# A fused attention and two-MLP kernel on one core: loads of the opening reordered, the scheduler's constants set anew, first copies of the seven products on two engines

## The chip, the cores and the metric

The kernel runs on one core of one Trainium2 chip. The metric is device time of one execution in microseconds (us), as the median of several runs.

## What is computed

```python
a = softmax(phi, axis=2)                        # phi: 4 batches, 8 heads, 576 rows, 32 memory slots
k_m = einsum('bhsm,bhsd->bhmd', a, k)           # k, v, q: 4, 8, 576, 64
v_m = einsum('bhsm,bhsd->bhmd', a, v)
attn = softmax(q @ k_m.T / sqrt(64)) @ v_m
x = attn.transpose(0, 2, 1, 3).reshape(2304, 512)
h = x @ w_in                                    # 512 x 2048
y = maximum(0.01 * h, h) @ w_out                # 2048 x 512
out = ((y @ w_a) * (y @ w_b)) @ w_out2          # 512 x 1536 twice, 1536 x 512
```

All of it is in fp32; softmax subtracts the row's maximum and adds 1e-9 to the sum.

## The kernel before

Every large matrix product runs on TensorE (PE) as three passes over operands that are split into a high and a low part (`hi` and `lo`). A weight arrives as 64-bit words; `weight` (to L525) loads it (L475, queue SP), turns it to fp32 in five passes (L481 and L484 on ACT, L488, L492, L496 and L499 on VectorE, DVE), and splits it: the high part is a copy (L404 or L406), the low part a subtraction (L505 on DVE, L387 on GpSimd, POOL).

The attention comes first. The batch index is b = 0 to 3, a head group g = 0 or 1 holds four heads, x = 0 or 1 is a half of 288 of the 576 rows. `kv_part(b, g)` loads phi, k with v (two tiles `kv` and a rest `kvr`), takes the softmax of phi (L555, L556, L559 and L560), transposes it (`ta`, `tz`), makes k_m and v_m (`km`), scales them (`kvn`, L595), transposes them (`kvt`) and sets them out (`kbd`, `vm_hi`, `vm_lo`). `q_load` loads q. `sc_part(b, g, x)` makes the scores (`sc`, L674), and on DVE their softmax: L680 (transposition), L688, L689, L693 to L695, L698, L699 (transposition back), then the split into `ahi` and `alo` (L705). `vw` multiplies v_m with w_in, so that the first MLP's h is the attention weights times `vw`, split again into `vwh` and `vwl` (L745, L772). The first MLP is in four chunks c of 512 columns; in each, `h_unit` makes h of block n (block n is batch n // 2, half n % 2) and leaky values `g` (L783, L822), and `y_unit` adds the products with w_out. The second MLP is in twelve chunks of 128 columns and two halves s of the rows; `ab_unit` makes its two products by seven products of half matrices, `o_unit` multiplies by w_out2. In half s = 1 the first eight chunks take w_out2 by seven products as well: `w2_sums` loads a tile `wf` (L1163) and makes sums of its quarters (`w2s`, `w2`), `p_sums` those of the other side (`pf`, `pT`, `pb`), and `o_part` multiplies (`os`, L1248). The results of the first pair of chunks are copied to seven tiles `osum`, each with two halves x (L404 on ACT or L406 on DVE), later ones are added.

The order of all this isn't written out. Every operation is handed to a `Program` with its engine (or several to choose from), its cost in us, what it reads and writes, and the tiles it holds. `urgency` goes back from the planned times of the main products and gives each operation a latest start, less its `slack`; `order` then places the operations one by one, on each engine the most urgent of those that are ready, and among several engines the one that would end first; `run` makes six rounds of that and keeps the shortest plan. `ahead` says how long before its latest start an operation may run, `keep` how many free slots must be left by it. Slots of 4 KB are handed out in that plan as well, 24 of them called `slot` and 20 called `big`; a load that takes a slot waits until its last reader is done, and a store is such a reader. `SLACK` holds the slacks by kind, `START` is the time planned for the first main product, `BIAS` is added to the cost of a copy on DVE. What comes out is five fixed lists of instructions, four engines and one queue of transfers (SP).

```python
def copy_by(n, psum=False):
    return (dict if psum else Port)({"ACT": c_act(n), "DVE": (c_dve(n) if psum else c_dve2(n)) + BIAS})
```

Of the kernel before, what the change touches and what calls it, by code (L numbers as in the profile page):

```python
# [19 lines left out]
P = 128  # L20
# [60 lines left out]
def c_dma(nbytes):  # L81
    return max(0.6, nbytes / 355e3)
# [250 lines left out]
def tile_mem_attention__leaky_mlp__bilinear_mlp(  # L333
# [128 lines left out]
    def weight(kind, c, k, after=()):  # L462
# [61 lines left out]
        op(copy_by(512), 0, hi, r=[a], w=[("hi", key)], tiles=[cv, key], ahead=any_time)  # L524
        op(two(512), 0, lo, r=[a, ("hi", key)], w=[key], tiles=[cv, key], ahead=any_time, slack=SLACK[kind + "0" if first else kind])  # L525


    def kv_part(b, g):
# [119 lines left out]
    def q_load(b, g):  # L648
# [584 lines left out]
    def o_part(q, x, nth, pos):  # L1233
# [151 lines left out]
```

## Time and profile before

| what | before |
|---|---|
| median of 3 runs | 809.02 us (807.88 to 809.16) |
| the profiled execution, own time | 809.07 us |
| its span in the trace | 807.3 us |
| PE busy | 784.9 us, 97% |
| DVE busy | 667.7 us, 83% |
| ACT busy | 375.8 us, 47% |
| POOL busy | 215.2 us, 27% |

The span is the time from the first to the last instruction of the trace; the execution's own time is 1.8 us longer. Busy time counts work only: an engine that waits for a transfer, or for another engine, is idle. Since PE does the bulk of the work in a fixed amount, its idle time is where time can be won, and what ended each piece of idle time is the question to ask of every view.

### The profile page before, as it was taken

How to read it: one execution, taken by the hardware profiler on the slowest of the kernel's cores; microseconds unless marked ns; L12 is line 12 of the kernel's file. 1: busy time of each engine (PE TensorE's matmuls, PEld its weight loads, DVE VectorE, ACT ScalarE, POOL GpSimd, SP SyncE). 2: the span in 40 equal slices, each digit the busy share in tenths (PEclk: the TensorE clock that was granted, in tenths of full speed). 3: DMA queues.
4: the chain of work that ended last, by engine and by line, in shares of the span. 5: the costliest groups of instructions: out<-in, count | busy, mean ns of one | idle time of the engine just before them, and what ended most of it. 6: DMA issues, size and time to landing. Idle time of an engine off the chain costs nothing.

```text
span 807.3 us, 13391 instructions
## 1 busy us (share of the span) xinstructions
PE 784.9 (97%) x4898; PEld 700.0 (87%) x4898; DVE 667.7 (83%) x1273; ACT 375.8 (47%) x817; POOL 215.2 (27%) x328
## 2 busy tenths in 40 slices
PE   5889999999999999999999999999999989999998
PEld 4578889999999999999988888888888878878886
DVE  6898899889887988888768899889885676888975
ACT  5657776777565665654326534344321143222110
POOL 3462247215011411431100113056330000244300
PEclk9789999999999999999999999999999999999999
DMA  9885302064227133136887555646578778957302
GB/s 325 323 281 181 132 1 74 6 235 125 76 76 267 59 132 118 42 125 233 279 311 276 209 199 192 208 158 202 216 264 304 276 267 274 296 173 283 130 1 104
DMA packets 55218, 150.02 MB, mean 186 GB/s; under 512 B 6897, under 2 KB 20209, under 8 KB 55153
## 3 DMA queue, kind: packets, MB, share of 16 engines
q1 hardware_dynamic: 55152, 149.18, 53.4%
q8 instruction: 38, 0.62, 0.3%
q14 instruction: 28, 0.22, 0.1%
HBM read 103.55 MB, written 45.61 MB: 185 GB/s over the span
## 4 chain that ended last, share of the span: by engine, by line
PE 93%; DMA 3%; DVE 2%; issue 1%; ACT 0%; SPq 0%; DVEq 0%; ACTq 0%
PE y L836 26%; PE o L1132 13%; PE h L806 12%; PE aby L1049 12%; PE abz L1049 8%; PE abx L1049 8%; PE os L1248 4%; PE vw L757 2%; PE b L1100 2%; PE a L1100 2%; PE sc L674 1%; DMA kvr<-in_kv_rest_dram 1%; DMA k_wout<-wout 1%; PE km L586 1%; DMA raw_win<-in_w_in_dram 1%
## 5 line engine op out<-in xcount | busy, mean ns | idle before, releaser
L836 PE MATMUL y<-g,wout 128*128 128x288 f32 x1536 | 221.0, 297 | 0.0
L836 PEld LDWEIGHTS y<-g,wout 128*128 128x128 f32 x1536 | 210.8, 190 | 3.7 <-issue 1.7
L1049 PE MATMUL aby<-yb_T,wo 128*128 128x512 f32 x432 | 110.2, 390 | 0.5 <-DVE t L1057 0.5
L1049 PEld LDWEIGHTS aby<-yb_T,wo 128*128 128x128 f32 x432 | 80.1, 188 | 16.8 <-DVE t L1057 0.9
L1132 PE MATMUL o<-p,wout 128*128 128x512 f32 x384 | 94.0, 390 | 0.0
L783 ACT ACTIVATE g<-h 128x288 fp32r<-128x288 f32 x128 | 52.8, 413 | 70.1 <-PE h L806 64.4
L1132 PEld LDWEIGHTS o<-p,wout 128*128 128x128 f32 x384 | 71.9, 188 | 15.4 <-DVE osum L1145 0.3
L806 PE MATMUL h<-ahi,vwh 128*128 128x288 f32 x256 | 76.8, 300 | 1.2 <-ACT ahi L404 1.2
L1057 DVE TENSOR_TENSOR t<-aby,t 128x512 f32<-128x512 f32 x72 | 49.5, 688 | 34.2 <-PE aby L1049 32.4
L806 PE MATMUL h<-alo,vwh 128*128 128x288 f32 x256 | 76.1, 297 | 0.8 <-POOL alo L387 0.8
L806 PE MATMUL h<-ahi,vwl 128*128 128x288 f32 x256 | 75.9, 296 | 0.0
L1049 PE MATMUL abx<-yb_B,wo 128*128 128x512 f32 x288 | 73.4, 390 | 0.0
L1049 PEld LDWEIGHTS abx<-yb_B,wo 128*128 128x128 f32 x288 | 53.4, 188 | 10.6
L848 DVE TENSOR_TENSOR acc<-y,acc 128x288 f32<-128x288 f32 x96 | 43.2, 454 | 19.6 <-PE y L836 18.7
L822 DVE TENSOR_TENSOR g<-t,g 128x288 fp32r<-128x288 f32 x102 | 49.0, 484 | 4.5 <-ACT t L783 4.4
L783 ACT ACTIVATE t<-h 128x288 f32<-128x288 f32 x128 | 52.4, 409 | 0.1
L806 PEld LDWEIGHTS h<-ahi,vwh 128*128 128x128 f32 x256 | 48.4, 189 | 4.2 <-issue 2.6
L806 PEld LDWEIGHTS h<-alo,vwh 128*128 128x128 f32 x256 | 48.6, 190 | 1.3 <-POOL alo L387 1.2
L806 PEld LDWEIGHTS h<-ahi,vwl 128*128 128x128 f32 x256 | 48.5, 189 | 0.0
L387 POOL TENSOR_TENSOR g<-t,g 128x288 fp32r<-128x288 f32 x26 | 26.4, 1017 | 76.0 <-ACT t L783 58.6
L772 DVE TENSOR_TENSOR vwl<-vw,vwh 64x512 fp32r<-64x512 f32 (+1 forms) x64 | 39.8, 622 | 7.4 <-ACT vwh L404 5.9
L404 ACT CAST vwh<-vw 64x512 fp32r<-64x512 f32 (+2 forms) x62 | 31.6, 509 | 23.7 <-PE vw L757 13.8
(328 smaller groups left out, 1472.6 us busy)
## 6 DMA issues: line engine op xcount, KB each, us to landing
k_wo<-wo SPq DMA_DIRECT2D x32, 512.0 KB, 2.9
wo<-k_wo SPq DMA_DIRECT2D x32, 512.0 KB, 4.9
raw_wout<-in_w_out_dram SPq DMA_DIRECT2D x24, 512.0 KB, 4.5
raw_win<-in_w_in_dram SPq DMA_DIRECT2D x16, 512.0 KB, 5.7
kv<-in_kv_dram SPq DMA_DIRECT2D x16, 512.0 KB, 8.5
k_yb_T<-yb_T SPq DMA_DIRECT2D x8, 512.0 KB, 7.9
raw_wa<-in_w_a_dram SPq DMA_DIRECT2D x8, 512.0 KB, 4.3
raw_wb<-in_w_b_dram SPq DMA_DIRECT2D x8, 512.0 KB, 5.9
```

The source lines that it names most:

```text
L404: nc.scalar.copy(dst, src)
L772: nc.vector.tensor_tensor(T[lk][to, j // 2, cols], T[o][i * 64:(i + 1) * 64, :], T[hk][to, j // 2, cols].bitcast(F32), op=ALU.subtract)
L783: nc.scalar.activation(dst, src, AF.Prelu, alpha=0.01)
L806: nc.tensor.matmul(T[o], T[w[u]][:, k, fs], T[a[v]][:, k, cols], start=(k == 0 and i == 0), stop=(k == 1 and i == 2))
L822: lambda T, e: engines[e].tensor_tensor(T[g][:, i, 1, :], T[t], T[g][:, i, 0, :].bitcast(F32), op=ALU.subtract),
L836: nc.tensor.matmul(T[o], w[:, u, es], g[:, v, :], start=(f == 0 and i == 0), stop=(f == 3 and i == 2))
L848: "DVE", c_dve(NB), lambda T: nc.vector.tensor_tensor(T[acc][:, e, :], T[o], T[acc][:, e, :], op=ALU.add),
L1049: nc.tensor.matmul(T[o], T[w][:, which, u, k * P:(k + 1) * P], T[ys[v]][:, k, :], start=first and k == 0 and x == 0, stop=k == 1 and x == ...
L1057: op("DVE", 0.69, lambda T: nc.vector.tensor_tensor(T[to], T[o], T[x], op=ALU.add), r=[o, x], w=[to], tiles=[o, x, to])
L1100: nc.tensor.matmul(T[o], T[w][:, k // 2, u, k % 2 * P:(k % 2 + 1) * P], T[ys[v]][:, k, :], start=(k == 0 and x == 0), stop=(k == 3 and x = ...
L1132: nc.tensor.matmul(T[o], T[w][:, u, es], T[g][:, at, v, :], start=(x == 0 and k == 0), stop=(x == 1 and k == 2))
L1248: nc.tensor.matmul(T[o], lhs(T, u), T[g][:, v, :], start=k == 0, stop=k == 2)
```

## The change

It sets `SLACK` and `START` anew, gives the loads of phi, kv, kvr and q of batch 0 slacks of their own (before, 0), gives the low halves of the first w_in and w_out one slack for each pair of tiles, lets the loads of batch 0 take the last free slots (`keep` 0 in place of 6), and drops `BIAS` from the cost that the scheduler sees for the first copies of the seven products on DVE.

```diff
-SLACK = {'win0': 5.37, 'wout0': 8.13, 'win': 4.9, 'wout': 4.64, 'wa': 23.6, 'wb': -0.15, 'wout2': 16.8, ...
-START = 17.4
+SLACK = {'phi0': 14.82, ('kv0', 0): -4.36, ('kv0', 1): 11.12, 'kvr0': 6.44, ('q0', 0): 2.5, ('q0', 1): 1.24, ...
+START = 22.2
...
-        op(two(512), 0, lo, ..., slack=SLACK[kind + "0" if first else kind])
+        op(two(512), 0, lo, ..., slack=SLACK[(kind + "0", k // 2) if first else kind])
...
-            op("DMA", c_dma(P * S * 4), lambda T: nc.sync.dma_start(T[phi], ...), w=[("e", b, g)], tiles=[phi])
+            op("DMA", c_dma(P * S * 4), lambda T: nc.sync.dma_start(T[phi], ...), w=[("e", b, g)], tiles=[phi], slack=SLACK["phi0"])
...
-            op("DMA", c_dma(P * 4096), ..., w=[k], tiles=[k], keep=6)
+            op("DMA", c_dma(P * 4096), ..., w=[k], tiles=[k], keep=6 if b else 0, slack=0 if b else SLACK["kv0", g])
...
-            op("DMA", c_dma(64 * 4096), ..., w=[rest], tiles=[rest], keep=6)
+            op("DMA", c_dma(64 * 4096), ..., w=[rest], tiles=[rest], keep=6 if b else 0, slack=0 if b else SLACK["kvr0"])
...
-            op("DMA", c_dma(P * S * 4), ..., w=[q], tiles=[q])
+            op("DMA", c_dma(P * S * 4), ..., w=[q], tiles=[q], slack=SLACK["q0", x])
...
         if q == 0:
-            op(copy_by(NB2, True), 0, lambda T, e: copy(e, part(T, i), T[o]), r=[o], w=[tok(i)], tiles=[o, acc(i)])
+            op({"ACT": c_act(NB2), "DVE": c_dve(NB2)}, 0, lambda T, e: copy(e, part(T, i), T[o]), r=[o], w=[tok(i)], tiles=[o, acc(i)])
             return
```

The lists that come out hold the same work in another order on all five. DVE has 1234 rows where it had 1262, POOL 182 where it had 147 (six low halves of `wo` and some of `g`, clamps and sums have moved there). SP began with four tiles of w_in, two phi, four kv, kvr, two q; it now begins with two phi, the two kv of g = 1, two tiles of w_in, kvr, the other two of w_in, the two kv of g = 0, and the two q. After them come phi of batch 1 and w_out, as before. Of the fourteen first copies (L404 or L406) three are now on DVE.

The first place is DVE's list where the opening ends, ahead of the first y. In the names, `sm_0_0_1` is the softmax tile of batch 0, g = 0, x = 1 (then `sm_0_1_1` is g = 1), `mx` its maxima, `wout_0_1` a tile of w_out with its low half written by L505, and the last number only counts. Before:

```order
L688 TENSOR_REDUCE mx_0_1_84<-sm_0_0_1_481 128x9
L688 TENSOR_REDUCE mx_1_1_86<-sm_0_1_1_485 128x9
L559 TENSOR_SCALAR kst_1_0_78<-kst_1_0_78 128x1
L560 RECIPROCAL kst_1_0_78<-kst_1_0_78 128x1
L559 TENSOR_SCALAR kst_1_1_79<-kst_1_1_79 128x1
L560 RECIPROCAL kst_1_1_79<-kst_1_1_79 128x1
L689 TENSOR_TENSOR sm_0_0_1_481<-sm_0_0_1_481,mx_0_1_84 128x288
L689 TENSOR_TENSOR sm_0_1_1_485<-sm_0_1_1_485,mx_1_1_86 128x288
L595 TENSOR_SCALAR kvn_1_0_575<-km_1_0_488,kst_1_0_78 128x256
L595 TENSOR_SCALAR kvn_1_1_579<-km_1_1_523,kst_1_1_79 128x256
L505 TENSOR_TENSOR wout_0_1_521<-cv_wout_0_1_333,wout_0_1_521 128x512
L505 TENSOR_TENSOR wout_0_2_545<-cv_wout_0_2_387,wout_0_2_545 128x512
```

Now:

```order
L559 TENSOR_SCALAR kst_1_1_79<-kst_1_1_79 128x1
L560 RECIPROCAL kst_1_1_79<-kst_1_1_79 128x1
L595 TENSOR_SCALAR kvn_1_0_529<-km_1_0_460,kst_1_0_78 128x256
L595 TENSOR_SCALAR kvn_1_1_533<-km_1_1_493,kst_1_1_79 128x256
L505 TENSOR_TENSOR wout_0_0_491<-cv_wout_0_0_324,wout_0_0_491 128x512
L505 TENSOR_TENSOR wout_0_1_516<-cv_wout_0_1_344,wout_0_1_516 128x512
L505 TENSOR_TENSOR wout_0_2_520<-cv_wout_0_2_367,wout_0_2_520 128x512
L505 TENSOR_TENSOR wout_0_3_531<-cv_wout_0_3_387,wout_0_3_531 128x512
L680 STREAM_TRANSPOSE sm_0_0_1_576<-sc_0_0_1_526 128x288
L680 STREAM_TRANSPOSE sm_0_1_1_584<-sc_0_1_1_535 128x288
L627 TENSOR_TENSOR vm_lo_110<-kvt_1_0_539,vm_hi_109 64x2x32 x2
L688 TENSOR_REDUCE mx_0_1_84<-sm_0_0_1_576 128x9
```

The x = 1 softmax of batch 0 (L680, L688, L689, two of each) stood ahead of kvn and of the low halves of w_out; it now stands behind them. Two of the four low halves were on POOL, now all four are on DVE.

The second place is DVE's list ahead of block 3. `alo_1` from `at_1_1_1` is the last input of its h; `sm_2` and `at_2` belong to batch 2. Before, this row was the 148th:

```order
L699 STREAM_TRANSPOSE at_1_0_1_989<-sm_1_0_1_813 128x288
L698 TENSOR_TENSOR sm_1_1_1_911<-sm_1_1_1_911,sr_1_1_87 128x288
L406 CAST vm_hi_109<-kvt_2_1_991 64x2x32 x2
L699 STREAM_TRANSPOSE at_1_1_1_1012<-sm_1_1_1_911 128x288
L680 STREAM_TRANSPOSE sm_2_0_0_1027<-sc_2_0_0_994 128x288
L705 TENSOR_TENSOR alo_1_824<-at_1_0_1_989,ahi_1_800 128x288
L688 TENSOR_REDUCE mx_0_0_80<-sm_2_0_0_1027 128x9
L705 TENSOR_TENSOR alo_1_824<-at_1_1_1_1012,ahi_1_800 128x288
```

Now it is the 164th:

```order
L698 TENSOR_TENSOR sm_2_0_0_990<-sm_2_0_0_990,sr_0_0_81 128x288
L698 TENSOR_TENSOR sm_2_1_0_1014<-sm_2_1_0_1014,sr_1_0_83 128x288
L699 STREAM_TRANSPOSE at_1_1_1_1143<-sm_1_1_1_873 128x288
L699 STREAM_TRANSPOSE at_2_0_0_1147<-sm_2_0_0_990 128x288
L699 STREAM_TRANSPOSE at_2_1_0_1162<-sm_2_1_0_1014 128x288
L559 TENSOR_SCALAR kst_1_0_78<-kst_1_0_78 128x1
L560 RECIPROCAL kst_1_0_78<-kst_1_0_78 128x1
L559 TENSOR_SCALAR kst_1_1_79<-kst_1_1_79 128x1
L560 RECIPROCAL kst_1_1_79<-kst_1_1_79 128x1
L705 TENSOR_TENSOR alo_1_869<-at_1_1_1_1143,ahi_1_837 128x288
```

The softmax of both head groups of batch 2, x = 0, stood behind this row and now stands ahead of it.

The third place is SP's list in the stage of the first seven products of w_out2, the second half of the second MLP. `k_wo_0_11_1<-wo_0_11_1` is a store of a weight tile, `wout2_2_1` and `wo_1_4_2` are loads, `wf_1` is the load that `w2_sums` waits for. Before:

```order
L1014 DMA k_wo_0_11_2_7777<-wo_0_11_2_7270 128x1024
L1014 DMA k_wo_0_11_3_7789<-wo_0_11_3_7297 128x1024
L1029 DMA wout2_2_1_7813<-k_wout2_2_-1_4382 128x1024
L1014 DMA k_wo_0_11_1_7825<-wo_0_11_1_7241 128x1024
L1163 DMA wf_1_7843<-k_wf_1_4324 128x1024
L1029 DMA wo_1_4_2_7859<-k_wo_0_4_2_5727 128x1024
L1014 DMA k_wout2_10_0_7874<-wout2_10_0_7342 128x1024
L1014 DMA k_wout2_11_0_7894<-wout2_11_0_7352 128x1024
```

Now:

```order
L1029 DMA wo_1_4_0_7803<-k_wo_0_4_0_5955 128x1024
L1014 DMA k_wo_0_11_3_7821<-wo_0_11_3_7348 128x1024
L1029 DMA wout2_2_1_7839<-k_wout2_2_-1_5175 128x1024
L1014 DMA k_wo_0_11_1_7854<-wo_0_11_1_7284 128x1024
L1163 DMA wf_1_7867<-k_wf_1_5116 128x1024
L1014 DMA k_wout2_10_0_7889<-wout2_10_0_7323 128x1024
L1014 DMA k_wout2_11_0_7903<-wout2_11_0_7342 128x1024
L1029 DMA wo_1_4_2_7923<-k_wo_0_4_2_5975 128x1024
```

The two stores `k_wout2` went out behind the load `wo_1_4_2` and now go directly behind `wf_1`. In the plan of slots, `wf_1` now takes the slot of `wo_0_11_1`, whose store stands one row ahead of it, the load `wout2_2_1` takes a slot that the matmuls `os_0_1_1` read last, and the copies of `os_0_0_7` and `os_0_1_7` go into the slot of `wout2_10`.

## Rows read from the trace of the kernel before

**Rows 1.** Busy time by stretch: length, then busy us (instructions) per engine, granted clock, transfers' share, GB/s.
```profile
0.00:50.00 50.00, 34.15 (x280) 24.27 (x281) 39.66 (x92) 29.94 (x72) 25.84 (x57) 0.82 0.87 303
...
70.00:650.00 580.00, 579.96 (x3772) 535.15 (x3765) 491.95 (x947) 296.05 (x645) 151.82 (x208) 1.00 0.49 172
...
660.00:680.00 20.00, 17.82 (x77) 14.27 (x77) 11.86 (x19) 9.00 (x16) 0.43 (x1) 1.00 0.80 260
...
sum 807.30, PE 784.85 PEld 700.03 DVE 667.75 ACT 375.76 POOL 215.23; mean PE 98.11 PEld 87.50 DVE 83.47 ACT 46.97 POOL 26.90
```

(The engines stand in the order PE, PE's weight load, DVE, ACT, POOL.)

**Rows 2.** Waits of PE: for what, us in total, times, longest.
```profile
PE kvt L603 <- DVE kvn L595: 2.4, 1, 2.4
...
PE os L1248 <- ACT osum L404: 2.2, 2, 1.5
```

**Rows 3.** Chain of waits, opening: start, length, what.
```profile
45.65 0.41 DVE kvn L595
...
48.53 4.99 PE y L836 x24
53.52 1.12 PE sc L674 x8
```

**Rows 4.** Timeline of DVE, opening: start, length, what it does, how often.
```profile
7.82 0.42 DVE L492 TENSOR_SCALAR cv_win<-cv_win 128x512 int32<-128x512 int32 x1
...
8.49 0.68 DVE L496 SCALAR_TENSOR_TENSOR cv_win<-raw_win,cv_win 128x512 int32<-128x512 int32 x1
...
33.30 2.65 DVE L492 TENSOR_SCALAR cv_wout<-cv_wout 128x512 int32<-128x512 int32 x4
35.87 3.68 DVE L496 SCALAR_TENSOR_TENSOR cv_wout<-raw_wout,cv_wout 128x512 int32<-128x512 int32 x4
...
40.08 0.83 DVE L680 STREAM_TRANSPOSE sm<-sc 128x288 f32<-128x288 f32 x2
...
43.15 0.80 DVE L688 TENSOR_REDUCE mx<-sm 128x9 f32<-128x288 f32 x2
...
44.37 1.28 DVE L689 TENSOR_TENSOR sm<-sm,mx 128x288 f32<-128x288 f32 x2
...
46.36 1.53 DVE L505 TENSOR_TENSOR wout<-cv_wout,wout 128x512 fp32r<-128x512 f32 x2
...
54.61 0.42 DVE L689 TENSOR_TENSOR sm<-sm,mx 128x288 f32<-128x288 f32 x1
```

**Rows 5.** Timeline of DVE and PE ahead of block 3.
```profile
64.87 0.45 DVE L688 TENSOR_REDUCE mx<-sm 128x9 f32<-128x288 f32 x1
...
70.12 1.06 DVE L698 TENSOR_TENSOR sm<-sm,sr 128x288 f32<-128x288 f32 x1
...
84.48 0.40 PE L806 MATMUL h<-ahi,vwh 128*128 128x288 f32 x1
```

**Rows 6.** Timeline of the os stage; brackets: idle before, and what ended it.
```profile
647.71 0.84 PE L1248 MATMUL os<-pb_B,wout 128*128 128x512 f32 x3
...
651.69 0.43 SPq L1014 DMA_DIRECT2D k_wo<-wo  x1
...
652.22 0.38 SPq L1163 DMA_DIRECT2D wf<-k_wf  x1
...
662.83 0.62 ACT L404 CAST w<-w2s 128x512 fp32r<-128x512 f32 x1 [2.03 <-DMA k_wout<-wout]
...
664.70 0.98 PE L1248 MATMUL os<-pb_B,wout 128*128 128x512 f32 x3 [1.50 <-ACT osum L404]
```

**Rows 7.** Transfers issued from 648 to 662 us: KB each, median us to landing.
```profile
k_wout<-wout SPq DMA_DIRECT2D x2, 512.0 KB, 8.7
...
k_wo<-wo SPq DMA_DIRECT2D x1, 512.0 KB, 5.3
wf<-k_wf SPq DMA_DIRECT2D x1, 512.0 KB, 6.2
```

**Rows 8.** Transfers of the whole program, by the page: columns as in rows 7.
```profile
k_wo<-wo SPq DMA_DIRECT2D x32, 512.0 KB, 2.9
```

More of the change, by code (lines that the diff above doesn't have):

```diff
@@ L52 @@
 LEAD = 12
-SLACK = {'win0': 5.37, 'wout0': 8.13, 'win': 4.9, 'wout': 4.64, 'wa': 23.6, 'wb': -0.15, 'wout2': 16.8, ('sc', 0, 0): 6.2, ('sc', 0, 1): 3.3, ('sc', 1, 0): 8.05, ('sc', 1, 1): 6.75, ('sc', 2, 0): 11.99, ('sc', 2, 1): 9.96, ('vw', 0, 0): 19.04, ('vw', 0, 1): 7.99, ('vw', 0, 2): 9.35, ('vw', 1, 0): -0.31, ('vw', 1, 1): 19.18, ('vw', 1, 2): 8.18}
-START = 17.4
+SLACK = {'phi0': 14.82, ('kv0', 0): -4.36, ('kv0', 1): 11.12, 'kvr0': 6.44, ('q0', 0): 2.5, ('q0', 1): 1.24, ('win0', 0): 5.4, ('win0', 1): 10.87, ('wout0', 0): 8.13, ('wout0', 1): 8.13, 'win': 10.62, 'wout': -1.7, 'wa': 16.21, 'wb': -3.23, 'wout2': 21.86, ('sc', 0, 0): 6.2, ('sc', 0, 1): 0.02, ('sc', 1, 0): 5.97, ('sc', 1, 1): 4.79, ('sc', 2, 0): 14.21, ('sc', 2, 1): 11.87, ('vw', 0, 0): 14.2, ('vw', 0, 1): 11.73, ('vw', 0, 2): 7.46, ('vw', 1, 0): 3.8, ('vw', 1, 1): 9.86, ('vw', 1, 2): 3.39}
+START = 22.2
 BIAS = 0.5
@@ L524, in weight @@
         op(copy_by(512), 0, hi, r=[a], w=[("hi", key)], tiles=[cv, key], ahead=any_time)
-        op(two(512), 0, lo, r=[a, ("hi", key)], w=[key], tiles=[cv, key], ahead=any_time, slack=SLACK[kind + "0" if first else kind])
+        op(two(512), 0, lo, r=[a, ("hi", key)], w=[key], tiles=[cv, key], ahead=any_time, slack=SLACK[(kind + "0", k // 2) if first else kind])
     def kv_part(b, g):
@@ L534, in kv_part @@
             tile_of(phi, "slot", [1, S])
-            op("DMA", c_dma(P * S * 4), lambda T: nc.sync.dma_start(T[phi], phiT[b, :, g:g + 1, :]), w=[("e", b, g)], tiles=[phi])
+            op("DMA", c_dma(P * S * 4), lambda T: nc.sync.dma_start(T[phi], phiT[b, :, g:g + 1, :]), w=[("e", b, g)], tiles=[phi], slack=SLACK["phi0"])
         elif g == 0:
@@ L547, in kv_part @@
             tile_of(k, "slot", [2, 512])
-            op("DMA", c_dma(P * 4096), lambda T, i=i, k=k: nc.sync.dma_start(T[k], kv[b, g, :, 2 * i:2 * i + 2, :]), w=[k], tiles=[k], keep=6)
+            op("DMA", c_dma(P * 4096), lambda T, i=i, k=k: nc.sync.dma_start(T[k], kv[b, g, :, 2 * i:2 * i + 2, :]), w=[k], tiles=[k], keep=6 if b else 0, slack=0 if b else SLACK["kv0", g])
         if g == 0:
             tile_of(rest, "slot", [2, 512], parts=64)
-            op("DMA", c_dma(64 * 4096), lambda T: nc.sync.dma_start(T[rest], kv_rest[b]), w=[rest], tiles=[rest], keep=6)
+            op("DMA", c_dma(64 * 4096), lambda T: nc.sync.dma_start(T[rest], kv_rest[b]), w=[rest], tiles=[rest], keep=6 if b else 0, slack=0 if b else SLACK["kvr0"])
         nmx, es, er = (stat(("kst", b % 2, g), 3)[:, i:i + 1] for i in range(3))
@@ L656, in q_load @@
             tile_of(q, "slot", [2, NB])
-            op("DMA", c_dma(P * S * 4), lambda T, q=q, cols=cols: nc.sync.dma_start(T[q], qT[b, g, :, :, cols]), w=[q], tiles=[q])
+            op("DMA", c_dma(P * S * 4), lambda T, q=q, cols=cols: nc.sync.dma_start(T[q], qT[b, g, :, :, cols]), w=[q], tiles=[q], slack=SLACK["q0", x])
     NM = NB // 32
```

## The prediction, made before the changed kernel ran

> **What bounds the kernel now.** I read the windows first. TensorE (PE) is busy for 784.85 of 807.3 us, and from 70 to 650 us for 579.96 of 580 [rows 1]: no order of the same instructions can gain anything there, it can only lose. What a new order can win lies in 22.4 us of idle PE: 15.85 in the first 50 us, 2.2 between 660 and 680, the rest in small pieces and in the tail [rows 1]. The list of waits names what ends the late ones: kvt waited 2.4 for DVE's kvn, and os waited 2.2 in two waits for a copy on ACT [rows 2]. The chain of waits then shows what the first 50 us hang on: DVE's kvn of batch 1 at 45.65, then PE's transposes, one sc product, and the first y at 48.53 [rows 3]. The rows of DVE before it have no gap [rows 4], though DVE is busy for only 39.66 of those 50 us [rows 1], so it is short of time at the end of the opening and has some to spare at its start. The profiled execution took 809.07, the median of the runs is 809.02; sums are made against 809.07, and the two are the same for this purpose. 0.2% is 1.6 us, about what a measurement of this kernel can tell from no change.
>
> **The change, part by part.** No instruction's work is new. The table, START and the changed costs alter the order on every engine, and for some operations the engine.
>
> Loads. phi, two kv and two win tiles go ahead of the other two win; before, four win stood first. The first thirteen transfers are the same set, so the last of them, q, lands when it did. Term: 0 by itself. Cost: DVE's conversions begin when a win lands as fifth instead of first. Two phi of 0.29 MB and two kv of 0.52 MB are 1.6 MB, and at the 303 GB/s of the first 50 us [rows 1] that is 5.3 us later. It is paid from DVE's 10.3 idle us [rows 1], which lie in waits for transfers and for km; the km of one head group now come earlier. I take the end of the first softmax (x = 0, block 0) as unmoved. If only half of the 5.3 is covered, 2.6 are lost; this makes the low bound.
>
> First y. It needs four low halves of wout, and kvt and sc of batch 1. Before, six instructions of the x = 1 softmax of batch 0 stood on DVE ahead of the low halves: L680 0.83, L688 0.80, L689 1.28, together 2.91 [rows 4]. The order now has them behind. Two low halves, before on POOL, are now with the others on DVE: two cost 1.53 [rows 4]. The last low half ended at 46.36 + 1.53 = 47.89; now 47.89 - 2.91 + 1.53 = 46.5. The first y can start there instead of at 48.53 [rows 3]: 2.0 earlier. PE also has one sc product more behind it by then, half of the 1.12 for two at 53.52 [rows 3], so 0.6 more. Lead: **2.6**. Here POOL matters: four L492 took 2.65 and four L496 3.68 while POOL worked, against 0.42 and 0.68 for one alone at 7.82 and 8.49 [rows 4], 1.0 and 1.0 lost. If the new order misses that collision, the lead is 4.6, the high bound.
>
> The lead has to be kept. The next place where DVE sets the pace is the h of block 3 (batch 1, x = 1), which ran at 84.48 [rows 5]. Its last input, the alo of that block, stood in row 148 of DVE's order and now stands in row 164, behind the x = 0 softmax of batch 2. From L688 of batch 1, which before ran at 64.87 [rows 5], to this alo there are now 42 rows: 22 of 288 columns at about 0.44, eight tiny ones at 0.2, two L595 at 0.47, four pairs at 0.46, two L555 at 0.7 and two short pairs at 0.32: 16.0 us. From 64.87 that is 80.9, or 82.1 with two of them at the 1.06 that L698 took at 70.12 [rows 5]. With a hop to PE the h starts at about 82.5 and not at 84.48, with 0.6 us of PE work less behind it than before, an sc product having been done early: 2.6 again, just held by DVE. I take **2.5** for the opening, bounds 0 (2.6 less 2.6) and 4.6.
>
> What speaks against this change: L492 at 0.42 alone and 2.65 for four beside POOL, and L689 at 0.42 against 1.28 for two [rows 4], show DVE held up while POOL runs. The Trainium skill, "SBUF — State Buffer", section "Who interferes with whom", says that DVE and GpSimd share one pair of ports as an exclusive lock, so that an instruction of DVE with two operands from SBUF blocks for the whole of a GpSimd instruction that reads there. The trace agrees in kind. By that rule the new order, which has 182 instead of 147 rows on POOL, would pay more on DVE than single rows add up to; what this would do here is rival B.
>
> os stage. Before, PE waited 2.2 us for copies on ACT [rows 2], the longer part at 664.70 behind a cast at 662.83 that waited 2.03 for the store of wout2's slot [rows 6]. Now the load wf_1 takes the slot of a wo tile whose store is issued just before it, and must wait for that to land. The load of wout2 ahead of both now waits for the os matmuls that ended at 647.71 + 0.84 [rows 6], so the store goes at about 649.2 instead of 651.69 [rows 6]. It lands 2.9 (the median of 32 stores [rows 8]) to 5.3 us (the one in this stretch [rows 7]) later, at 652.1 to 654.5, against wf's issue at 652.22 before [rows 6]; wf takes 6.2 [rows 7]. The store of wout2 follows and takes up to 8.3 to 8.7 [rows 7], and the copy of os_0_0_7 now goes into that slot: slowest 654.9 + 8.3 + 0.6 = 663.8, where PE arrives at about 660.0: 3.8 of stall instead of 2.2. Fastest, with both stores near the median, the copy waits for nothing. Bounds -1.6 and +2.2. I take **+0.8**, nearer the fast end, because wf's issue time falls on both sides of the old one and the cast no longer stands between.
>
> First copies of the seven products. BIAS is gone from their cost, yet in the order only three of the fourteen move from ACT to DVE. ACT is far from full there; 0 but for what stands above.
>
> The rest. Between 70 and 650 PE idled 0.04 us [rows 1]; the new order there can only add. I put it at 0, cover being the buffers that keep PE fed; bound -1.
>
> Sum: 809.07 - 2.5 - 0.8 = **805.8**.
>
> **Rivals.** *A, the os stage gives the gain back.* wf_1 and the copy wait for two slow stores, as in the bound: 809.07 - 2.5 + 1.6 = 808.2. For it: the two prices measured in this stretch are 5.3 and 8.7 [rows 7]. Against it: 2.9 is the median [rows 8], and the store goes out earlier.
>
> *B, slower: DVE becomes the bound at h of block 3.* Ten instructions of the stretch read two operands (three L689, three L698, two pairs L627, one L705, one L822). If each meets POOL and takes 1.06 instead of 0.44, 16.0 becomes 22.2 and the alo comes at 87.1, h at 87.4. It decides from the point at which h starts after 84.48 + 0.6 = 85.1. Lead -2.3: 811.4, or 810.6 with the os gain; I enter 811. For it: rows 148 to 164, and 35 rows more on POOL. Against it: the same kinds stand there at their single prices too, 0.42 for L689 at 54.61 [rows 4].
>
> *C, more.* Both high bounds: 809.07 - 4.6 - 2.2 = 802.3. It needs a collision with POOL to vanish and fast stores.
>
> *D, the change doesn't do what it says.* As the loads of the first weights stand behind 1.6 MB of phi and kv, the opening may simply be the same length, DVE being late by what it was early: that is the low bound 0, 808.3 with the os gain, and cannot be told from no change.
>
> **How the numbers follow.** Forecast 0.58, A 0.14, B 0.14, C 0.08, D 0.06. Faster by over 0.2% is forecast and C: 0.66. Within: A and D: 0.20. Slower: B: 0.14. The range runs from near C to near B, 802.5 to 810.8; outside it lie half of C and half of B with their tails, some 0.15.
>
> **What would show it.** In the profile after: the first y near 46.5 instead of 48.53; h of block 3 near 82.5; PE busy for some 36 us of the first 50 instead of 34.15 [rows 1]; full PE from 70 to 650; os waits near 1.4. Wrong it would be if PE waits appear between 60 and 100 us for alo (B), if os waits exceed 3.5 (A), or if the first y hasn't moved (D).

## The result: slower by 1.1%, and the profile after

The changed kernel takes 816.65 us (median of 4 runs, 815.62 to 818.59), the kernel before 808.45 in the runs beside it: a ratio of 1.0108, 95% interval 1.0086 to 1.0129. The prediction was 805.8, faster; the time is outside its range, 802.5 to 810.8. A second series of the unaltered kernel gave 1.0101 (1.0082 to 1.0121).

The profiled execution of the changed kernel took 815.71, 6.6 more than that of the kernel before. The windows are read first again; they answer to [rows 1], with two stretches of 20 us more (columns as there):

```profile
0.00:50.00 50.00, 33.53 (x289) 24.58 (x290) 38.11 (x87) 30.47 (x75) 26.41 (x54) 0.76 0.90 306
70.00:650.00 580.00, 572.11 (x3706) 527.00 (x3706) 481.09 (x910) 295.93 (x645) 198.91 (x282) 1.00 0.48 167
660.00:680.00 20.00, 18.94 (x81) 14.81 (x81) 14.61 (x24) 9.98 (x18) 0.79 (x1) 1.00 0.85 287
...
sum 813.90, PE 784.84 PEld 699.67 DVE 666.82 ACT 375.77 POOL 260.94; mean PE 98.10 PEld 87.46 DVE 83.35 ACT 46.97 POOL 32.62
...
420.00:440.00 20.00, 15.09 (x57) 11.33 (x56) 8.88 (x17) 7.43 (x13) 0.00 (x0) 0.91 0.78 271
440.00:460.00 20.00, 18.44 (x106) 16.10 (x105) 12.71 (x25) 8.99 (x18) 1.12 (x1) 1.00 0.86 307
```

PE's busy sum is the same, 784.84 against 784.85, so the two executions differ by PE's idle time. From 70 to 650, where it was 0.04, it is 7.89, and 6.47 of that lies between 420 and 460, near the start of the second MLP, far from every place that the prediction looked at. The same windows of all three kernels that matter in the end (`slots_all` comes below), as idle time of PE in us, length less busy:

| stretch | before | after | slots_all |
|---|---|---|---|
| 0 to 70 | 16.09 | 16.47 | 17.14 |
| 70 to 390 | 0.04 | 1.42 | 1.43 |
| 390 to 460 | 0 | 6.47 | 0.05 |
| 460 to 650 | 0 | 0 | 0.17 |
| 650 to 790 | 2.63 | 1.06 | 0 |

The differences, after minus before, add up to 6.66, the 6.6 of the two executions. That the busy sums are equal is a balance of two things, as one group of PE's rows shows (before, then after: busy time, mean ns, idle time):

```profile
L1132 PE MATMUL o<-p,wout 128*128 128x512 f32 x384 | 94.0, 390 | 0.0
L1132 PE MATMUL o<-p,wout 128*128 128x512 f32 x384 | 96.4, 395 | 4.9 <-ACT p L404 4.6 <-DVE p L790 0.2
```

The same 384 products took 2.4 us longer. Behind the 4.6 us in which PE had no work, the granted clock was 0.74 from 425 to 430 and 0.91 from 430 to 435, so part of that time at 1.2 GHz instead of 2.4; in the kernel before it was 1.00 there. PE had got as much back earlier: up to 421 us, where both orders have done the same matmuls, its busy time is 2.4 less. Part of that is seen from 45 to 50, where the granted clock was 0.52 in the kernel before, behind the wait of 2.4 for kvn, and is 1.00 now. At 421 us PE was thus 0.7 us ahead of the kernel before, at 470 it was 8.5 behind: the stall cost about 9 us, 6.5 of it idle time.

The list of PE's waits gives the large one a name (it answers to [rows 2]):

```profile
PE o L1132 <- ACT p L404: 4.6, 1, 4.6
...
PE h L806 <- POOL alo L387: 2.6, 1, 2.6
PE o L1132 <- ACT oaccl L404: 1.6, 1, 1.6
...
PE kvt L603 <- DVE kvn L595: 1.0, 1, 1.0
...
PE os L1248 <- ACT pb_T L404: 0.7, 1, 0.7
```

The wait for kvn went from 2.4 to 1.0 (with 0.4 more for a softmax tile), and the waits in the os stage went from 2.2 to 0.9 (0.7 and 0.2, now for pb_T), so the waits that the change was read for did get shorter. The new one is for a cast on ACT. The timeline of ACT and PE there (brackets: idle before, and what ended it) shows that ACT itself was waiting, for a weight:

```profile
425.79 0.66 ACT L484 ACTIVATE cv_wa<-raw_wa 128x512 int32<-128x512 uint32 x1 [9.91 <-DMA raw_wa<-in_w_a_dram]
426.36 0.60 ACT L404 CAST p<-t 128x512 fp32r<-128x512 f32 x1
427.01 0.50 PE L1132 MATMUL o<-p,wout 128*128 128x512 f32 x1 [4.59 <-ACT p L404]
```

The cast of p, 0.60 us long, stands in ACT's list behind a conversion of the next chunk's w_a, and ACT had idled 9.91 us for the load of that weight. Why was the load late? The queue SP issues in order; its timeline, each row an issue:

```profile
398.52 0.42 SPq L1014 DMA_DIRECT2D k_wo_-1_3_3_5411<-wo_-1_3_3_5216  x1
407.72 0.32 SPq L1029 DMA_DIRECT2D wo<-k_wo_-1_2_3_4533  x1
...
408.56 0.43 SPq L1014 DMA_DIRECT2D k_wo_-1_3_1_5462<-wo_-1_3_1_5067  x1
415.62 0.32 SPq L1029 DMA_DIRECT2D wo<-k_wo_-1_3_0_4941  x1
416.00 0.42 SPq L1014 DMA_DIRECT2D k_wout_-1_5480<-wout_-1_5144  x1
...
421.82 0.38 SPq L475 DMA_DIRECT2D raw_wa<-in_w_a_dram  x1
```

and its waits from 395 to 425:

```profile
SPq L1029 <- DMA k_wo_-1_3_3_5411<-wo_-1_3_3_5216: 8.8, 1, 8.8
...
SPq L1029 <- DMA k_wo_-1_3_1_5462<-wo_-1_3_1_5067: 6.6, 1, 6.6
SPq L475 <- DMA k_wout_-1_5480<-wout_-1_5144: 4.5, 1, 4.5
```

Three times a store of a weight tile (`k_...<-`) goes out, and the load in the next row or the row after takes the 4 KB slot that this store is still reading. The load waits until the store has landed, 4.5 to 8.8 us, and all behind it in the queue waits too: 19.9 us of the 23 from 398.9 to 421.8. The third of those loads is the w_a that ACT waits for. A fourth pair, with a wait of 8.7, stands just ahead of the three. In the kernel before, the stores of the same chunk, number 3, stood elsewhere:

```profile
334.23 0.33 SPq L1014 DMA_DIRECT2D k_wo_-1_3_0_4537<-wo_-1_3_0_4468  x1
...
348.69 0.32 SPq L1014 DMA_DIRECT2D k_wo_-1_3_2_4738<-wo_-1_3_2_4586  x1
...
362.66 0.32 SPq L1014 DMA_DIRECT2D k_wout_-1_4921<-wout_-1_4857  x1
...
414.49 0.38 SPq L475 DMA_DIRECT2D raw_wa<-in_w_a_dram  x1
```

Five stores between 334 and 363 us became five between 364 and 416, the last three of them among the loads with which the second MLP begins, and the same load of w_a goes out at 421.82 instead of 414.49. The plan sees none of this: it prices a store of 512 KB by its share of bandwidth, some 1.8 us, and hands its slot out at the end of that. The plan's own length is 798.8 with the change and 802.1 without: to the scheduler the changed order is the shorter one.

How often this could happen can be counted in the plan that the kernel makes: tiles that take a slot whose store was begun less than 6.25 us before. There are 21 in the kernel before, 9 of them loads; in the changed one 35, 15 of them loads.

### The profile page after: what moved, and what is told of

It reads as the page before. It is cut to its first block, busy times and chain, and to the rows that moved or that the text cites. A ratio compares the mean times of both kernels' runs of the same rounds, so it can differ in the third digit from the quotient of the medians.

```text
span 813.9 us, 13431 instructions
## 1 busy us (share of the span) xinstructions
PE 784.8 (96%) x4898; PEld 699.7 (86%) x4898; DVE 666.8 (82%) x1245; ACT 375.8 (46%) x818; POOL 260.9 (32%) x395
## 4 chain that ended last, share of the span: by engine, by line
PE 84%; DMA 9%; DVE 4%; issue 1%; ACT 1%; POOL 1%; SPq 0%; DVEq 0%; ACTq 0%
PE y L836 23%; PE o L1132 12%; PE h L806 12%; PE aby L1049 10%; PE abz L1049 7%; PE abx L1049 7%; PE os L1248 4%; DMA kv<-in_kv_dram 3%; PE vw L757 2%; PE b L1100 2%; PE a L1100 2%; PE km L586 1%; PE sc L674 1%; DMA k_wo_-1_3_3_5411<-wo_-1_3_3_5216 1%; DMA k_wo_-1_3_1_5462<-wo_-1_3_1_5067 1%; DMA k_wo<-wo 1%
## 5 line engine op out<-in xcount | busy, mean ns | idle before, releaser
L1132 PE MATMUL o<-p,wout 128*128 128x512 f32 x384 | 96.4, 395 | 4.9 <-ACT p L404 4.6
L848 DVE TENSOR_TENSOR acc<-y,acc 128x288 f32<-128x288 f32 x96 | 43.2, 453 | 21.1 <-PE y L836 20.4
L387 POOL TENSOR_TENSOR g<-t,g 128x288 fp32r<-128x288 f32 x32 | 29.3, 921 | 45.8 <-ACT t L783 42.5
L404 ACT CAST p<-t 128x512 fp32r<-128x512 f32 x31 | 19.1, 620 | 47.4 <-DVE t L1078 23.7
```

The source lines that it names most:

```text
L387: nc.gpsimd.tensor_tensor(dst[x], a[x], b[x], op=op)
L848: "DVE", c_dve(NB), lambda T: nc.vector.tensor_tensor(T[acc][:, e, :], T[o], T[acc][:, e, :], op=ALU.add),
L1132: nc.tensor.matmul(T[o], T[w][:, u, es], T[g][:, at, v, :], start=(x == 0 and k == 0), stop=(x == 1 and k == 2))
```

## The experiments

All times are medians of the series named, and each ratio is to the kernel before, run beside it. Where an edit adds lines, the kernel's lines stand four further down.

| run | what | median (runs) | ratio, 95% interval |
|---|---|---|---|
| after_again | the changed kernel again | 816.45 (6) | 1.0101, 1.0082 to 1.0121 |
| slots_mid | three loads in other slots, same lists | 810.67 (12) | 1.0030, 1.0014 to 1.0045 |
| slots_mid_again | the same | 811.49 (12) | 1.0037, 1.0022 to 1.0052 |
| a_vw10 | one number of the table as before | 808.15 (12) | 1.0001, 0.9988 to 1.0014 |
| a_keep5 | five kept slots instead of eight | 808.50 (12) | 1.0012, 1.0000 to 1.0025 |
| b_opening | before, with the loads' part alone | 812.27 (7) | 1.0046, 1.0029 to 1.0063 |
| b_copies | before, with the copies' cost alone | 806.97 (12) | 0.9987, 0.9972 to 1.0001 |
| b_copies_again | the same | 806.65 (12) | 0.9991, 0.9977 to 1.0006 |
| a_vw10_oldloads | a_vw10, loads in the old order | 807.84 (12) | 0.9997, 0.9983 to 1.0011 |
| a_vw10_clamp | a_vw10, two clamps on DVE | 807.43 (12) | 0.9996, 0.9984 to 1.0007 |
| a_keep5_oldcopies | a_keep5, old cost of copies | 811.86 (5) | 1.0058, 1.0042 to 1.0074 |
| a_keep6_clamp | six kept slots, clamps on DVE | 810.82 (5) | 1.0045, 1.0031 to 1.0060 |
| slots_430 | slots_mid and one load more | 818.44 (6) | 1.0130, 1.0107 to 1.0154 |
| slots_wide | slots_mid and two loads more | 816.06 (6) | 1.0107, 1.0082 to 1.0131 |
| slots_wide_again | the same | 813.69 (6) | 1.0065, 1.0040 to 1.0090 |
| slots_wide_third | the same | 816.90 (1) | one execution, no interval |
| slots_all | no just-stored slots, same lists | 806.27 (12) | 0.9975, 0.9960 to 0.9989 |
| b_copies_slots | the same rule on b_copies | 803.35 (6) | 0.9939, 0.9921 to 0.9956 |

**Is it the slots?** `slots_mid` leaves all five lists of the changed kernel as they are. For a short time of the plan, three loads take slots that no store has just left:

```diff
-                    mine = mine or big
+                    mine = ([t for t in mine if t not in stored] or [t for t in big if t not in stored] if 395 < now < 415 else []) or mine or big
```

(`stored` holds the slots whose last user was a store.)

> The changed kernel with every engine's list kept as it is; only between 395 and 415 us of the plan three loads (wo_0_2_3, wo_0_3_0, raw_wa_4) take slots other than the ones whose last reader is a store issued one to two rows ahead. Theory (the changed kernel loses at 420 to 460 us because loads wait on SP for late stores of the kept weights to land, and ACT and PE wait for the last of these loads): PE's wait of 4.6 us at 427 and the slow stretch up to 437 go, idle PE in 400 to 500 falls from 6.5 to under 2 us, time 809 to 811.5. Rival (the transfers of this stretch are simply too many for the queues): the load of raw_wa still lands near 425, time 815.5 to 817.5.

6.0 us of the loss came back with no instruction moved. In its profile PE is full where it had stalled, and ACT waits 3.77 for w_a instead of 9.91 (timeline of ACT, then windows of the kernel):

```profile
421.68 0.66 ACT L488 ACTIVATE cv_wa<-raw_wa 128x512 int32<-128x512 uint32 x1 [3.77 <-DMA raw_wa<-in_w_a_dram]
```

```profile
420.00:440.00 20.00, 20.00 (x101) 17.04 (x100) 15.51 (x28) 10.77 (x19) 1.12 (x1) 1.00 0.86 297
440.00:460.00 20.00, 17.80 (x90) 15.54 (x90) 10.48 (x21) 7.83 (x16) 2.63 (x4) 0.91 0.74 260
```

The 2.2 that are left lie at 450, a little over the expected 2. (This profile is of the longest of the twelve executions, 814.12; it also idles 18.2 us in the first 70, where the changed kernel's idled 16.5.) The unaltered kernel, run once more, kept its wait of 4.6 us and its time:

> The changed kernel once more, unaltered, beside the others of this call on the same chip. If its loss is the stall at 420 to 460 us, every profile of it shows 5 us or more of idle PE between 400 and 500; time 815 to 818. The lead at 100 us, 2.2 in its first profile, -0.1 and -1.4 in the two other kernels whose lists are the same up to there, will fall between -1.5 and 2.5: it hangs on when the first kv lands.

**Which number of the change brings it?** The stores are late because the loads of chunk 3's weights are: they may start only while eight slots are free (`keep`), and with the new table that is so later. Two edits of the changed kernel, one number each, move those stores forward:

```diff
-('vw', 1, 0): 3.8
+('vw', 1, 0): -0.31
```

> The changed kernel with one number of its table put back: ('vw', 1, 0) -0.31 in place of 3.8. In the plan the five stores of chunk 3's kept weights then go 20 to 45 us earlier. Theory: this number, not the opening and not the copies, makes the weights of the kept chunks late, so the stall at 420 to 440 goes; time 807 to 811, the gains of the opening and of the os stage showing. Rival (the stall belongs to the new opening or to the table as a whole): PE idles 4 us or more between 400 and 500 as before, time 814 or more.

```diff
-        op("DMA", c_dma(524288), load, ..., keep=8 if early else 2 if late else 7 if c < 2 else 4)
+        op("DMA", c_dma(524288), load, ..., keep=5 if early else 2 if late else 7 if c < 2 else 4)
```

> The changed kernel with one number altered, and not one of the table: the loads of the kept weights may start with 5 free slots left in place of 8. Theory (the new table leaves fewer slots free, so these loads, their conversions and their stores come late): the stores then fall at 250 to 330 us of the plan, nothing waits for one at 420, idle PE of 400 to 500 under 1 us, time 806.5 to 810. Rival (the stall comes from ACT or DVE doing too much there, whenever the stores go): 813 or more.

Both end at the time of before; each takes away some 8 us. In `a_keep5` the last store of chunk 3 goes out 82 us earlier than in the changed kernel (there at 416.00), and PE has no gap (timeline of SP, then window):

```profile
333.57 0.32 SPq L1014 DMA_DIRECT2D k_wo_-1_3_3_4611<-wo_-1_3_3_4484  x1
```

```profile
400.00:500.00 100.00, 100.00 (x531) 86.47 (x530) 82.69 (x145) 44.63 (x84) 16.91 (x23) 1.00 0.67 233
```

That a slack of `vw` decides when loads of the second MLP start is the scheduler's doing; that it does so by the count of free slots is argued from `a_keep5`, not shown step by step.

**What are the parts worth?** The loads' part alone, on the kernel before, loses:

```diff
-SLACK = {'win0': 5.37, 'wout0': 8.13, 'win': 4.9, ...
+SLACK = {'phi0': 14.82, ('kv0', 0): -4.36, ('kv0', 1): 11.12, 'kvr0': 6.44, ..., 'win': 4.9, ...
...
+ keep=6 if b else 0, slack=0 if b else SLACK["kv0", g]
```

> The kernel before with the opening's part of the change alone (slacks and keep of the loads of batch 0, slacks of the low halves of the first w_in); table, START and copies as before. Theory: lead of 2 to 3 us by 70 us that stays to the end, no stall at 420; time 805.5 to 807. Rival 1: the opening by itself gains nothing (808 to 809.5), what is seen at 60 to 120 us in the changed kernel comes from the sc and vw numbers. Rival 2: it carries the late stores: 812 or more.

The old slacks of sc keep the x = 1 softmax ahead of kvn and of the low halves, and the loads are later, so both costs add (waits of PE, then timeline of DVE, where kvn was at 45.65 [rows 3]):

```profile
PE kvt L603 <- DVE kvn L595: 4.5, 3, 2.8
```

```profile
41.93 0.83 DVE L680 STREAM_TRANSPOSE sm<-sc 128x288 f32<-128x288 f32 x2
...
48.52 0.86 DVE L595 TENSOR_SCALAR kvn<-km,kst 128x256 f32<-128x256 f32 x2
```

PE idles 21.1 us in the first 70, 5.0 more than in the kernel before, and is full from 400 to 500. So the time is rival 2's, but not for rival 2's reason, late stores.

With the new slacks of sc the order of the loads is worth nothing that can be measured: `a_vw10` with the old order of loads runs within the interval of `a_vw10`.

```diff
-'phi0': 14.82, ('kv0', 0): -4.36, ('kv0', 1): 11.12, 'kvr0': 6.44, ('q0', 0): 2.5, ('q0', 1): 1.24, ('win0', 0): 5.4, ('win0', 1): 10.87
+'phi0': 0.0, ('kv0', 0): 0.0, ('kv0', 1): 0.0, 'kvr0': 0.0, ('q0', 0): 0.0, ('q0', 1): 0.0, ('win0', 0): 5.37, ('win0', 1): 5.37
...
-keep=6 if b else 0
+keep=6
```

> The changed kernel with ('vw', 1, 0) -0.31 (which took the stall away) and with the loads of batch 0 in their old order; the numbers for sc and vw stay new. Theory (the new order of loads brings q 2 to 3 us later and gains nothing; what it gave in the forecast came from the softmax of x = 1 going behind the low halves): 805 to 807.3. Rival (the new loads are what makes the opening shorter, as the prediction had it): 809.5 to 811.

The 807.84 lies between the two ranges, so it decides for neither.

The wait for alo of 2.6 in the opening is new as well. It follows four clamps of w_out on POOL; with two of them put on DVE it fell to 0.5, and the time by 0.7, which two intervals that overlap don't separate.

```diff
-        op(Port({"DVE": 0.42, "POOL": 2.45}), 0, clamp, w=[a], tiles=[cv], ahead=any_time)
+        op(Port({"DVE": 0.42, "POOL": 2.45}), 0, clamp if (kind, c) != ("wout", 0) else lambda T, e: clamp(T, "DVE"), w=[a], tiles=[cv], ahead=any_time)
```

> The changed kernel with ('vw', 1, 0) -0.31 and every list as it then is, except that two clamps of the first w_out are done by DVE and not by POOL, where they stood ahead of the first alo. Theory (DVE sets the first y, PE's wait of 2.2 us for alo at 37 is free time): the wait goes, the first y does not come earlier, time 807.3 to 809. Rival (the wait for alo is on the path): 805 to 806.7.

The copies' cost alone, on the kernel before:

```diff
-            op(copy_by(NB2, True), 0, ...)
+            op({"ACT": c_act(NB2), "DVE": c_dve(NB2)}, 0, ...)
```

> The kernel before with the changed costs of the fourteen first copies alone; up to 640 us every list is the same as before. Theory: the gain of the changed kernel at 660 to 720 us (1.9 us of PE idle less) is of these copies: os waits for copies on ACT go from 2.2 to under 1, time 806.3 to 807.8. Rival: the gain came with the other slots of the changed plan, the copies alone give nothing: 808 to 809.3.

> The kernel before with the changed costs of the first copies alone, a second time, for its interval: 0.9987 (0.9972 to 1.0001) the first time. If the gain is real the second ratio lies between 0.997 and 0.9995; if it was chance, at 1.000 or above.

About 0.1% faster twice, each interval just reaching no change. The os waits don't bear the theory out: they are 0.3 us in the first profile, but 2.9 in the second (an execution of 808.82). One execution of the second series took 2212 us; the ratio leaves it out. Taken out of `a_keep5`, the same line cost 3.4 us, in the rival's direction and past its range:

```diff
-            op({"ACT": c_act(NB2), "DVE": c_dve(NB2)}, 0, ...)
+            op(copy_by(NB2, True), 0, ...)
```

> The changed kernel with the kept weights' loads at 5 free slots, and the fourteen first copies at their old costs; up to 640 us the same lists as with the new costs. In that kernel (808.5) PE lost 1.6 us at 650 to 660 and 1.6 at 680 to 720 to pb_T. Theory (what the copies' costs are worth depends on the stores and slots around them, 0.9 us in the kernel before): within 1.5 us of 808.5, os waits of another kind. Rival (the new costs are a gain wherever they stand): 809.3 to 810.5.

Of the 2.4 us by which the two profiles differ, only 0.7 are idle time of PE from 650 to 790. The other 1.7 are idle time of the first 70 us, where the lists are the same, so the 3.4 are not shown to be the price of this line.

A last mixture, six kept slots with the clamps on DVE, missed what was expected of it: PE waited 2.1 for a value of ACT between 390 and 420.

> The changed kernel with the kept weights' loads at 6 free slots in place of 8, and the two clamps of the first w_out on DVE. Theory: the stores at 335 to 380 us of the plan are early enough, no wait at 420, and the clamps are worth up to 0.7: 806 to 808.5. Rival (6 is not enough, the stall comes back in part): 810 or more.

**Is it the slots everywhere?** The rest of `slots_mid`'s loss, at 450, looked like the same thing: in its queue the loads of w_b and w_a waited 5.3 and 4.0 us for stores of yb tiles. The next kernels give other slots for longer, lists untouched:

```diff
-395 < now < 415
+395 < now < 460
```

> The changed kernel with the lists of all five queues untouched, and the other slots given in the plan from 395 to 460 us instead of 395 to 415. Beside the three loads of slots_mid, wb of chunk 4 (its load waited 5.3 us behind the store of a yb tile in the profile of slots_mid) and the second w_out2 load of chunk 5 take slots that no store has just left; the load of wa of chunk 5 keeps its slot, there being no other, and its wait of 4.0. Theory (the second stall, at 450 to 460, is of the same kind as the first: a load behind the store of its own slot): raw wb of chunk 4 is issued some 4 us earlier, PE's wait for oaccl of 2.2 goes, PE idles under 1.0 us from 400 to 500, and the time is 807.5 to 809.5, 1 to 3 under slots_mid's 810.67. Rival (the second stall is transfers in each other's way, or the later loads are late from other causes): PE still waits 2 us or more between 440 and 460, and the time stays at 810 to 811.5.

> slots_mid unaltered, beside slots_wide_again on one chip. If the gain of the three other slots is real, the median is 809.5 to 812 once more, PE has no wait over 1 us between 400 and 440, and the runs spread by no more than 6 us. If it was a matter of that chip or hour, it comes out near 816, as slots_wide did.

> slots_wide unaltered, to get a profile of a usual run: its profile was of the shortest run, 810.7, the other five took 813.3 to 818.5. Theory: each run has one or the other stall, for the five longer ones a load that is late between 390 and 470 in a place where the profiled one just made it; the profile then shows PE with 3 to 6 us of waits in one place between 390 and 470. Rival: the longer runs lose their time elsewhere (opening, os stage), and 400 to 500 shows under 1 us idle at 813 us or more.

```diff
-395 < now < 415
+395 < now < 430
```

> The changed kernel with the same lists and other slots given from 395 to 430 us of the plan: slots_mid and, beside it, wb of chunk 4 in a slot that no store has just left (slots_wide also moves a w_out2 load of chunk 5). Theory: wb of chunk 4 is issued near 421 instead of 425, and PE has no wait over 1 us between 440 and 460. Time 807.5 to 809.5 if the profile of slots_wide is typical of it, 813 to 817 if what makes slots_wide long is this load's new slot.

`slots_mid` repeated. The other two were surprises: in every profile of them the stalls at 420 and 450 were gone, or down to 0.9 us, and yet the medians were 813.7 to 818.4. The windows of `slots_430` show why:

```profile
650.00:790.00 140.00, 132.05 (x567) 108.12 (x566) 109.92 (x172) 33.11 (x56) 29.32 (x47) 0.98 0.60 203
400.00:500.00 100.00, 100.00 (x532) 86.51 (x531) 79.49 (x140) 43.50 (x82) 16.11 (x22) 1.00 0.85 294
```

From 400 to 500 PE is full; from 650 to 790 it idles 7.95 us where the changed kernel idled 1.06. A slot given differently at 420 changes who gets which slot to the end, and in the os stage new pairs of store and next user came up. PE's waits of that kernel, and ACT's from 640 to 730:

```profile
PE os L1252 <- ACT pb_T L408: 5.3, 1, 5.3
...
PE os L1252 <- ACT osum L408: 2.7, 1, 2.7
```

```profile
ACT pb_T L408 <- DMA out_dram<-oacc: 8.6, 1, 8.6
```

A cast of pb_T was given the slot of a result tile on its way out, and ACT stood 8.6 us. `slots_wide` has the same in a milder and less steady form, with runs from 810.5 to 818.5 in its two series. Its three profiles, of executions of 810.7, 814.8 and 816.9 us, idle 0, 0.2 and 0.95 us from 400 to 460, and 3.2, 4.3 and 3.7 from 650 to 790. The third is of one execution by itself:

> slots_wide once more, one look, for a third profile: the same two outcomes as in slots_wide_again.

So the test had to cover the whole rest of the program. `slots_all` is the changed kernel, its five lists untouched, with this rule:

```diff
-                    mine = mine or big
+                    mine = ([t for t in mine if now - stored.get(t, -99) > 6] or [t for t in big if now - stored.get(t, -99) > 6] if 330 < now < 900 else []) or mine or big
```

> The changed kernel with the lists of all five queues untouched; from 330 us of the plan to its end a tile takes a slot that a store left less than 6 us before only if there is no other. In the changed kernel's plan 35 tiles take such a slot, 18 of them by loads; here 17 do, and after 330 us none of them is a load. Theory (the loss is nothing but such slots, and each of slots_wide and slots_430 only moved some of them to the os stage): PE idles under 1 us from 400 to 500 and no more than 3 from 650 to 790, and the time is 806 to 809.5, 7 to 10 under the changed kernel. Rival (the order itself is at fault, its stores of chunk 3 being late in whatever slots): it stays over 811, with the waits in yet another place.

(That text counts 18 loads among the 35; there are 15.) The time is 806.27, 10 us under the changed kernel, and 0.25% under the kernel before. Its windows:

```profile
400.00:500.00 100.00, 99.95 (x531) 86.21 (x530) 78.21 (x139) 41.31 (x77) 13.97 (x18) 1.00 0.83 285
...
650.00:790.00 140.00, 140.00 (x620) 115.89 (x619) 117.39 (x183) 34.45 (x59) 29.49 (x47) 1.00 0.59 196
```

The stores of chunk 3 go out nearly as late as in the changed kernel, from 365 to 411 us, and the last four land 5.2 to 8.3 us after their issue, where it was 5.4 to 9.2. Only nobody waits for their slots: from 395 to 425 none of the queue's waits is for a store, the load of w_a goes out at 414.42 instead of 421.82, and ACT waits 2.29 for it (timelines of SP and ACT):

```profile
414.42 0.38 SPq L479 DMA_DIRECT2D raw_wa<-in_w_a_dram  x1
...
419.09 0.67 ACT L488 ACTIVATE cv_wa<-raw_wa 128x512 int32<-128x512 uint32 x1 [2.29 <-DMA raw_wa<-in_w_a_dram]
```

The profile is 9.4 us shorter than that of the changed kernel: 6.6 of idle time, and 2.8 of PE's busy sum, of which 2.2 are the 384 products of o (94.2 here). The order was sound, and the loss was the slots, all of it.

The same rule over the whole plan, on the kernel before with the copies' cost (`b_copies`), brings the 21 such tiles down to 2:

> The kernel before with the changed cost of the first copies (b_copies), its lists untouched, and the same rule for slots over the whole plan: 2 tiles instead of 21 take a slot that a store left less than 6 us before. Theory: what b_copies still waits for in the os stage goes as well, 804 to 806.5, 0.1 to 0.4% under the kernel before, with os waits under 0.5 in sum. Rival (those waits are covered in the kernel before, or the other slots bring waits for matmuls in place of those for stores): within 0.1% of it, 807 to 808.

```profile
650.00:790.00 140.00, 140.00 (x618) 115.54 (x618) 115.69 (x182) 34.46 (x58) 30.28 (x47) 1.00 0.59 196
```

803.35 us, 0.61% under the kernel before (0.44 to 0.79%): a version that beats both, by more than expected. Its os stage has no gap left, where the kernel before had 2.63.

## Why the prediction was wrong, and where it was right

**The step that failed** is "The rest": "Between 70 and 650 PE idled 0.04 us; the new order there can only add. I put it at 0, cover being the buffers that keep PE fed; bound -1". The new order added 7.85 us of idle time, and the lower clock behind the stall 2.4 more. The buffers were the weak point, not the cover: it is by waiting for a buffer that the queue lost its time. I had the mechanism at hand, for the very same thing is priced in the term for the os stage and is rival A: a load into the slot of a tile whose store is issued just before it. I looked for it where PE had idled before, and not where it had not, though the lists and the plan's slots of the new order could be read to their end. At the place that I priced, the queue waited for it but PE did not; 230 us ahead of it, where I didn't look, PE lost 6.5 us by it, and the 2.4 besides.

**Size of that wait.** The price that I took from the page, 2.9 us for a store to land [rows 8], is the median of the 32 stores of chunks 4 to 11. The stores that were waited for took 5.4 to 9.2 from issue to landing in the changed kernel, and there the 32 have this row on the page:

```profile
k_wo<-wo SPq DMA_DIRECT2D x32, 512.0 KB, 6.5
```

Same count, same bytes, more than twice the time. They go out later and closer together: 7 of the 32 before 460 us in the kernel before, none in the changed one. A landing time belongs to a place in the queue; the 5.3 of the one store in the os stage [rows 7] was nearer.

**The opening.** The DVE side came out as worked out: the four low halves end at 46.55 (forecast 46.5), two L680 follow them.

```profile
44.05 2.50 DVE L505 TENSOR_TENSOR wout<-cv_wout,wout 128x512 fp32r<-128x512 f32 x4
...
46.47 0.83 DVE L680 STREAM_TRANSPOSE sm<-sc 128x288 f32<-128x288 f32 x2
```

But the first y did not start there (timeline of PE):

```profile
46.99 0.44 PE L603 MATMUL kvt<-ident,kvn 128*128 128x128 f32 x2 [0.40 <-DVE sm L680]
47.40 1.19 PE L674 MATMUL sc<-q,kbd 128*64 128x288 f32 x8
48.52 1.75 PE L836 MATMUL y<-g,wout 128*128 128x288 f32 x11
...
83.15 0.40 PE L806 MATMUL h<-ahi,vwh 128*128 128x288 f32 x1
```

"The first y can start there" fails: a transposition kvt stands ahead of it on PE and needs a result buffer that the moved L680 frees, and then two sc products come first. The y is at 48.52 against 48.53 [rows 3], with an sc product more behind it. The h of block 3 came at 83.15, 1.3 earlier than before [rows 5], where 2.0 was forecast (82.5). "The last of them, q, lands when it did" was wrong too: q landed 1.8 to 3.2 us later in profiles with this order of loads. From 70 to 390 us PE then idled 1.42 in small pieces, 1.1 of it vw behind DVE's acc. PE was busy for 33.53 us of the first 50, and not some 36. At 421 us, where both orders have done the same matmuls, the changed one is 0.7 us ahead in its own profile, 0.1 behind in that of `after_again`, and from 2.2 ahead to 2.0 behind in the other seven with its lists; the mean of the nine is 0.1 behind. The 2.5 was thus not kept, but for most of it in one profile; rival D, which said that the opening would be the same length, describes this part best.

**The os stage** moved the way that was forecast, by more, and not as it was worked out: forecast 0.8 less, measured 1.57 less idle time from 650 to 790, and 2.63 with `slots_all`. The store ahead of wf_1 took 6.6 us to land, over the 5.3 that was the slow end, and both waits of the forecast's slow case came, for wf_1 and for the copy into the slot of wout2_10 (waits of SP and of ACT):

```profile
SPq L1163 <- DMA k_wo<-wo: 5.8, 1, 5.8
```

```profile
ACT osum L404 <- DMA k_wout<-wout: 2.9, 1, 2.9
```

PE met neither of them; the 0.9 us that it waited were for pb_T, which the forecast doesn't name. That the sign came out right was in part luck.

**Rival B** did not occur: with 261 us of POOL's work instead of 215, no wait of PE for alo lies near block 3. Of the Trainium skill's rule on the shared ports ("SBUF — State Buffer", section "Who interferes with whom"), which stood behind B, the trace shows nothing that decides: four low halves, each with two operands, took 2.50 in all with POOL at work from 45.32 on, 0.63 each against 0.77 for each of two before [rows 4].

**The number.** `slots_all`, which has the changed kernel's five lists and no such slots, takes 806.27, half a microsecond from the 805.8 that I forecast, but by another sum: the os stage gave more and the opening little. Its profile is 2.8 us shorter than that of the kernel before; at 421 us, the same matmuls done, it is still 0.25 behind, and the 2.8 come later, 2.6 of them as idle time that is gone from the os stage. That the number came so near is luck.

**What stays open:** why a_keep5 without the copies' cost is 3.4 slower, and what makes the runs of slots_wide differ by up to 8 us (of the 6.2 between the spans of its first and third profile 2.8 are idle time of PE and 3.4 its longer busy time). The first kv landed between 6.7 and 8.6 us in runs with the same lists, and such a shift moves all the later ones against each other; that this is the reason was not tried.

## What to carry to other kernels

A buffer that a store still reads is not free when the store is issued, and not after its bytes over the bandwidth either: here it was 5 to 9 us after the issue, and an in-order queue makes all the loads behind wait too. After any reordering, read the queue of transfers from end to end for a store followed by a user of its slot, above all where the main engine had no gap before, since a full engine has only something to lose. A planner that hands out slots should count the landing time before it calls a slot free. Here it passed over such slots for 6 us while another was free; that rule alone, without a moved instruction, was worth 10 us on the changed kernel and, with the copies' cost, 0.6% on the kernel before.

## What the runs showed of the hardware that I had not expected

The same 32 stores of 512 KB land after 2.9 us at the median in one order and after 6.5 in another, and single ones after 9.2. A stall of PE costs more than its idle time: behind the 4.6 us at 427 the granted clock was 0.74 for the next stretch, and the products of o took 2.4 us longer in all, which the equal busy sums of the whole program (784.84 and 784.85) hide. Two kernels with the same five lists, whose tiles lie in other slots and so wait for other stores, ran 12 us apart (`slots_all` 806.27, `slots_430` 818.44).
